# Cosine attention and highway layer: pair 5 and token tile 1 turned on TensorE, in a newly planned order

## The chip, the cores and the metric

The kernel runs on one core of a Trainium2 chip. The metric is the time of the whole kernel on the device in microseconds, the median of several runs. The engines are TensorE (PE in the profile; its weight loads are PEld), ScalarE (ACT), VectorE (DVE), GpSimd (POOL) and SyncE (SP), and 16 DMA engines move data.

## The reference

For 8 batches of 12 heads, 448 positions and 64 dimensions, queries and keys are divided by their norms, the scores divided by tau = 0.1 go through a softmax, and the result weighs v. The heads are then put side by side to 3584 tokens of 768 numbers, and a highway layer follows.

```python
q_n = q / (np.linalg.norm(q, axis=-1, keepdims=True) + 1e-06)
k_n = k / (np.linalg.norm(k, axis=-1, keepdims=True) + 1e-06)
scores = np.matmul(q_n, k_n.transpose(0, 1, 3, 2)) / tau
attn = softmax(scores)
x = np.matmul(attn, v).transpose(0, 2, 1, 3).reshape(3584, 768)
H = np.maximum(x @ w_h, 0.0)
T = 1.0 / (1.0 + np.exp(-(x @ w_t + b_t)))
out = T * H + (1.0 - T) * x
```

## The kernel before, in words

**Pairs and tiles.** Work is cut into 48 head pairs (pair n belongs to batch n // 6; heads n % 6 and n % 6 + 6 of it) and 28 token tiles of 128 tokens (three for each batch, and one more for every two batches, made of the last 64 positions of both). For each batch k, q and v are loaded by GpSimd's DMA with a cast to fp16 (names l, r, v, x; tiles raw, vf, vp). For batch 0 the first two pairs come sooner: as fp32, into the tile fa, by the queues of SyncE and ScalarE (op `fa`). The squares (`sq`, lines 607 and 608, on ScalarE or VectorE), the sums (`f1`, `f2`, `red`) and an inverse square root by VectorE (`nw`) give the factors. The products with them (`nm`, lines 667 and 668) write qkn, one instruction for each half of a pair, on VectorE or GpSimd.

**The turn of a pair.** For the scores a pair must lie with the dimensions in the partitions (qkT). There are two ways: seven transposes on TensorE into PSUM (`pt`, line 683) and a copy by ScalarE or VectorE (`cp`, lines 692 and 694), or one DMA transpose in SyncE's queue (`tr`, line 699). A token tile is turned in the same two ways before its matmuls with w_h and w_t: six transposes (`xp`, line 840) and a copy (`xc`, lines 848 and 850), or a DMA transpose (`xt`, line 832). The list CHOICES says which: 1 for TensorE, 0 for DMA. Its first 48 entries are the pairs, the other 28 the tiles.

**The rest of a pair.** Four groups of score matmuls (`qk`, lines 739 and 742), four exps on ScalarE (`ex`, lines 756 and 758), 32 matmuls with v (`av`, line 779; `vc`, lines 715 and 716, has spread v before), and the division on VectorE (`un`, lines 787 to 793) into xb, or st for the last 64 positions, which two small DMAs then bring into xl (`sh`). A tile's matmuls are `ff` (lines 864 and 867, two halves for each weight), then `d`, `t`, `g`, `h`, `e` and `o` combine them and `st` stores. The weights are loaded as halves `w00`, `w01` (w_h) and `w10`, `w11` (w_t).

**Fillers.** In the first microseconds there is nothing to multiply. Filler matmuls of 128x512 (line 485) on a constant tile zf keep TensorE busy; FILLS gives how many stand in each place (`fill0`, `fill1`, ...). The first two places together open the program.

**The order.** All ops are listed with `add`, and each has a number by its place in that list. QUEUES holds, for each engine, the numbers of its ops in the order in which it runs them, so that every instruction waits behind those before it. This order was made ahead of time by a planner (class Planner), which estimates how long an op takes, when a load lands and which buffers are free; the estimates for a DMA are the five entries of `dma`: its class, the number of units, the time of one, and the times before and after. HOLDS says for some of the loads which pair's first scores must have run before they begin. In the kernel before, some numbers are: pt0 207, pt1 212, tr5 234, qk5_0 527, av5 535, xt1 982, w00 to w11 22 to 25. With four places for fillers more, all later numbers rise by four.

In the order before, PE runs ... av3, qk5_0, qk4_2, qk4_3, av2, qk5_1 ..., and SP runs fa, the load of b_t, tr5, xt1, the first store, tr12 ... After the first two pairs' squares ScalarE takes one piece of batch 0's squares and copies pair 1, while VectorE copies pair 0 and squares the other piece.

Of the kernel before, what the change touches and what calls it, by code (L numbers as in the profile page):

```python
# [19 lines left out]
FILLS = [9, 23, 2, 8, 1, 1, 3, 6, 1, 1, 1, 1, 3, 1]  # L20
# [4 lines left out]
        1, 2, 207, 212, 3, 477, 479, 4, 487, 5, 489, 6, 481, 7, 491, 483, 8, 227, 493, 222, 485, 495, 217, 507, 517, 509, 9, 511,  # L25
        10, 497, 513, 11, 519, 12, 499, 13, 501, 503, 515, 527, 521, 523, 505, 529, 531, 533, 525, 242, 535, 547, 14, 237, 549,
        996, 965, 551, 553, 537, 247, 968, 539, 999, 541, 970, 557, 257, 543, 559, 561, 983, 252, 262, 972, 567, 985, 545, 569,
        555, 577, 987, 974, 579, 563, 571, 989, 587, 1001, 581, 573, 589, 565, 583, 591, 575, 593, 585, 595, 1003, 1042, 1005,
        1011, 1045, 597, 599, 1047, 1014, 601, 603, 607, 1049, 609, 617, 1016, 1030, 611, 619, 1032, 605, 647, 613, 621, 1018,
        1034, 649, 651, 1020, 1061, 623, 627, 629, 1063, 615, 637, 653, 639, 1036, 625, 631, 633, 641, 1051, 635, 677, 643, 657,  # L30
        655, 645, 659, 679, 1065, 1067, 1104, 661, 302, 681, 683, 322, 1107, 667, 663, 669, 1109, 665, 1111, 685, 687, 707, 1076,
        671, 673, 697, 1078, 709, 699, 675, 701, 703, 689, 1092, 1080, 711, 691, 693, 1094, 1082, 1096, 1098, 695, 1113, 713, 727,
        729, 705, 715, 737, 731, 733, 352, 1120, 1135, 747, 739, 735, 1138, 717, 719, 1140, 1123, 1125, 1127, 749, 721, 723, 1154,
        1129, 751, 757, 725, 767, 753, 1142, 1144, 741, 769, 743, 1169, 1171, 1173, 771, 773, 759, 1175, 1156, 761, 763, 745, 755,
        765, 775, 787, 789, 1158, 1182, 817, 777, 1197, 1160, 779, 819, 1185, 1200, 781, 797, 783, 1187, 1202, 791, 821, 1189,
        1216, 799, 801, 803, 785, 1218, 807, 809, 793, 1220, 1222, 811, 827, 795, 1191, 813, 829, 831, 805, 815, 887, 889, 823,
        1204, 833, 891, 825, 835, 837, 893, 839, 1206, 1244, 841, 843, 877, 895, 1247, 845, 1249, 857, 867, 1251, 1231, 847, 849,
        1253, 851, 853, 869, 1262, 859, 855, 871, 873, 861, 1278, 1280, 863, 879, 881, 1282, 1284, 865, 875, 883, 1264, 907, 909,
        885, 1233, 927, 929, 1235, 931, 933, 917, 1237, 919, 1266, 911, 921, 923, 1309, 1311, 1268, 913, 897, 899, 1293, 1295,
        947, 901, 903, 1297, 1324, 1299, 905, 915, 937, 939, 935, 949, 925, 941, 943, 951, 1313, 953, 945, 955, 1315, 1326, 1328,  # L40
        1330, 1355, 1357, 1340, 1342, 1344, 1371, 1346, 1359, 1361, 1373, 1375, 1377, 1386, 1388, 1391, 1393,
    ],
    "ACT": [
        29, 126, 134, 213, 478, 480, 488, 482, 445, 446, 490, 484, 492, 494, 228, 141, 518, 508, 510, 512, 498, 514, 520, 500,
        502, 504, 528, 522, 524, 530, 532, 534, 243, 548, 550, 966, 552, 554, 538, 540, 542, 558, 258, 560, 544, 253, 562, 973,
        451, 568, 155, 578, 988, 570, 975, 580, 564, 572, 990, 588, 582, 574, 590, 584, 453, 592, 594, 160, 1004, 164, 1006, 1012,
        598, 600, 602, 608, 604, 1050, 610, 618, 612, 620, 455, 622, 648, 1019, 1035, 614, 650, 1021, 652, 628, 624, 630, 638,
        640, 1037, 654, 632, 634, 1052, 642, 678, 644, 658, 458, 461, 680, 1066, 660, 1068, 662, 682, 684, 323, 664, 668, 173,
        670, 1112, 688, 708, 672, 698, 674, 710, 700, 702, 690, 704, 1081, 692, 712, 694, 1083, 1097, 1099, 1114, 714, 728, 730,
        738, 732, 734, 1136, 740, 748, 463, 718, 182, 720, 1128, 722, 724, 750, 1130, 752, 758, 464, 768, 1143, 754, 1145, 742,  # L50
        744, 770, 772, 1174, 1176, 774, 760, 762, 764, 187, 788, 790, 1159, 818, 778, 1198, 1161, 780, 820, 465, 466, 782, 798,
        792, 822, 784, 1190, 800, 802, 804, 467, 808, 810, 1221, 469, 794, 812, 828, 1223, 1192, 814, 830, 832, 888, 824, 834,
        1205, 890, 892, 838, 894, 840, 1207, 1245, 842, 844, 878, 200, 868, 858, 1252, 848, 850, 1254, 852, 854, 870, 860, 872,
        862, 874, 864, 880, 1283, 882, 1285, 884, 908, 910, 928, 930, 1236, 932, 918, 1238, 920, 934, 922, 912, 473, 924, 1267,
        1269, 474, 898, 900, 914, 475, 1298, 902, 904, 1300, 948, 938, 940, 950, 942, 944, 952, 954, 1314, 1316, 1329, 1331, 1345,
        1347, 1360, 1362, 1376, 1378, 1387, 1389,
    ],
    "DVE": [
        0, 20, 18, 21, 27, 127, 128, 129, 138, 210, 205, 206, 211, 208, 130, 131, 135, 136, 132, 137, 133, 139, 140, 220, 225,
        226, 221, 16, 215, 223, 145, 447, 218, 486, 142, 146, 448, 143, 147, 144, 149, 240, 496, 148, 506, 516, 246, 235, 526,  # L60
        536, 449, 238, 150, 997, 248, 250, 969, 450, 260, 251, 971, 261, 1000, 984, 263, 452, 151, 986, 152, 546, 153, 156, 991,
        157, 556, 976, 992, 977, 154, 993, 158, 994, 159, 1002, 566, 576, 586, 596, 271, 1043, 290, 161, 1046, 280, 281, 162,
        1015, 286, 454, 1048, 1007, 1008, 1053, 1054, 1017, 163, 165, 1031, 166, 1033, 167, 606, 168, 1022, 1023, 305, 1024, 1062,
        456, 315, 1064, 1025, 316, 616, 1038, 626, 311, 1039, 1055, 1040, 1056, 636, 457, 459, 646, 656, 460, 301, 1105, 1069,
        303, 1070, 1108, 169, 1110, 170, 666, 171, 174, 172, 175, 1077, 1115, 176, 1116, 177, 1079, 676, 335, 1093, 336, 686,
        1084, 1085, 1095, 351, 325, 345, 341, 326, 1100, 696, 1086, 462, 1101, 1087, 1117, 706, 716, 1118, 353, 1121, 178, 1139,
        179, 1141, 180, 1124, 1126, 183, 181, 184, 185, 1155, 186, 355, 726, 736, 1131, 1146, 1148, 1147, 1149, 1170, 1132, 1172,
        360, 356, 1177, 1178, 1179, 1157, 371, 1180, 746, 756, 766, 776, 191, 1183, 192, 188, 189, 1162, 1163, 190, 193, 1186,
        194, 1188, 1201, 195, 1203, 1217, 411, 385, 390, 786, 1219, 468, 405, 470, 471, 796, 472, 386, 406, 1224, 806, 1193, 816,
        1194, 1208, 826, 1209, 836, 196, 1225, 1210, 1211, 1226, 1248, 846, 1250, 197, 198, 201, 202, 199, 1232, 1255, 1256, 1263,  # L70
        203, 856, 204, 1279, 1281, 421, 430, 425, 431, 426, 866, 876, 1265, 440, 886, 415, 896, 441, 416, 1239, 1234, 1286, 1240,
        1241, 1242, 1310, 1312, 1270, 1271, 1272, 1273, 1287, 1294, 1296, 476, 1288, 1325, 1301, 1302, 1303, 906, 916, 1304, 926,
        936, 946, 956, 1327, 1317, 1332, 1333, 1318, 1356, 1358, 1334, 1341, 1343, 1335, 1348, 1372, 1363, 1364, 1374, 1365, 1366,
        1349, 1350, 1379, 1380, 1381, 1390, 1392, 1394, 1395, 1396,
    ],
    "POOL": [
        15, 17, 30, 37, 34, 38, 35, 31, 36, 32, 33, 42, 94, 96, 95, 44, 39, 43, 40, 97, 41, 45, 98, 25, 46, 216, 230, 231, 23, 22,
        100, 99, 53, 245, 241, 49, 236, 19, 24, 51, 48, 255, 256, 52, 47, 50, 101, 54, 60, 57, 58, 102, 104, 55, 105, 61, 56, 59,
        103, 978, 62, 68, 265, 266, 275, 270, 276, 69, 291, 285, 1009, 63, 65, 64, 110, 295, 66, 296, 306, 300, 106, 107, 320,
        310, 108, 70, 74, 67, 321, 109, 112, 71, 73, 111, 1071, 75, 78, 340, 77, 330, 331, 350, 83, 113, 76, 84, 72, 1102, 346,  # L80
        79, 81, 114, 82, 370, 80, 86, 375, 85, 115, 365, 361, 376, 366, 1133, 380, 381, 116, 118, 93, 120, 119, 117, 1164, 121,
        410, 89, 87, 92, 395, 400, 90, 401, 91, 88, 396, 1195, 391, 1257, 122, 420, 435, 436, 123, 124, 125, 1319,
    ],
    "SP": [
        28, 26, 234, 982, 995, 269, 957, 274, 279, 958, 294, 1029, 284, 979, 289, 1060, 299, 309, 1010, 1041, 1026, 959, 314,
        1057, 1075, 319, 1091, 1072, 339, 334, 329, 344, 1153, 349, 960, 1103, 1168, 1088, 1119, 364, 379, 359, 374, 369, 1181,
# [297 lines left out]
def kernel(  # L384
# [35 lines left out]
    fa = pool_.tile([128, 28, D], FP32, name="fa", tag="fa")  # L420
# [32 lines left out]
    add = P.add  # L453
# [586 lines left out]
```

## Time and profile before

| | before |
|---|---|
| time, median of 3 runs | 281.58 us (280.13 to 282.31) |
| profiled run: time, span | 279.94 us, 278.2 us |
| mean granted TensorE clock | 0.975 |
| busy share PE, PEld, DVE, ACT, POOL | 92%, 55%, 79%, 75%, 47% |
| chain that ended last | PE 71%, DMA 13%, ACT 6%, DVE 4% |
| DMA | 42.97 MB, mean 154 GB/s |
| fillers on TensorE | 61 matmuls, 18.2 us |
| DMA turns of pairs and of tiles | 34 and 18 |

The span is the time from the first to the last instruction. A share of an engine's busy time is a mean over all stages, so it doesn't say which engine sets the end in one of them. The chain is followed back from the last instruction, at each step to what released it; a DMA piece in it runs from issue to landing. Matmul ends are modelled, so TensorE can show as busy while it is paced by something else.

### The profile page before, as it was taken

Reading aid. Unit: us, or ns where it says so; the run is one execution under the profiler, and the core shown is the slowest. Engines: PE = TensorE matmul, PEld = TensorE weight load, DVE = VectorE, ACT = ScalarE, POOL = GpSimd, SP = SyncE. Lnnn points to the kernel's source line nnn. Section 1 sums busy time; section 2 is a strip of 40 time slices with the busy share of each in tenths; the row PEclk is TensorE's granted clock in tenths of the full one; section 3 lists DMA queues with packets and bytes.
Section 4 is the critical chain, followed back from the end, with each engine's and each line's share of the span. In section 5 each row is a group of like instructions: output and inputs, shape, how many; then the busy total and the mean of one; then the engine's idle time right before and its main releaser. Section 6 shows DMA issues by size and latency. Waiting matters only on the chain.

```text
span 278.2 us, 7772 instructions
## 1 busy us (share of the span) xinstructions
PE 255.8 (92%) x3155; PEld 153.3 (55%) x3155; DVE 219.0 (79%) x514; ACT 207.9 (75%) x287; POOL 131.2 (47%) x165
## 2 busy tenths in 40 slices
PE   7499729999999799999999999899999999999991
PEld 3135317556755367555765566356655655676660
DVE  3698935978999769799988989887798886756583
ACT  2359927899998869999599889888999589682230
POOL 9944731994856658148570778384303500001000
PEclk9979986999999999999999999999999999999997
DMA  8999695799999999999999999999855987514533
GB/s 165 183 182 173 92 181 65 112 183 182 141 149 179 159 210 170 213 134 193 145 120 191 199 157 135 174 154 161 213 128 128 192 107 192 130 59 91 171 152 113
DMA packets 109925, 42.97 MB, mean 154 GB/s; under 512 B 102721, under 2 KB 106305, under 8 KB 109890
## 3 DMA queue, kind: packets, MB, share of 16 engines
q0 software_dynamic: 56896, 18.42, 64.1%
q1 hardware_dynamic: 52162, 23.61, 38.2%
q8 instruction: 24, 0.39, 0.6%
q10 hardware_dynamic: 832, 0.46, 0.6%
q14 instruction: 11, 0.09, 0.1%
HBM read 37.75 MB, written 11.01 MB: 175 GB/s over the span
## 4 chain that ended last, share of the span: by engine, by line
PE 71%; DMA 13%; ACT 6%; DVE 4%; issue 2%; SPq 1%; POOL 1%; DVEq 0%; ACTq 0%
PE pb L864 33%; PE pb L779 17%; PE sc L739 11%; DMA xT<-xb 4%; DMA qkT<-qkn 4%; ACT ex L756 4%; PE sl L742 3%; DMA xT<-xl 3%; PE pb L867 3%; PE pb L683 2%; DMA fa<-in_k_dram 2%; PE pb L485 2%; ACT sq L607 1%; DVE sq L608 1%; PE pb L840 1%
## 5 line engine op out<-in xcount | busy, mean ns | idle before, releaser
L756 ACT ACTIVATE ex<-sc 128x896 f16<-128x896 f32 x144 | 127.7, 930 | 25.0 <-PE sc L739 23.2
L864 PEld LDWEIGHTS <-xT 128*128 128x128 f16 x672 | 60.8, 98 | 52.2 <-issue 13.1
L864 PE MATMUL pb<-w_h,xT 128*128 128x384 f16 x336 | 61.9, 327 | 2.5 <-DMA xT<-xl 1.7
L864 PE MATMUL pb<-w_t,xT 128*128 128x384 f16 x336 | 64.0, 327 | 0.0
L668 POOL TENSOR_TENSOR qkn<-raw,rs 128x448 f16<-128x448 f16 x44 | 40.7, 938 | 44.0 <-DVE qkn L668 18.3
L739 PE MATMUL sc<-qkT 64*64 64x448 f16 x576 | 50.7, 374 | 7.8 <-DMA qkT<-qkn 5.7
L779 PEld LDWEIGHTS <-ex 128*128 128x128 f16 x1536 | 52.5, 98 | 9.1 <-issue 7.6
L779 PE MATMUL pb<-vp,ex 128*128 128x65 f16 x1536 | 56.0, 194 | 0.2 <-ACT qkT L692 0.2
L951 POOL TENSOR_TENSOR o<-d,xb 128x768 f32<-128x768 f16 x8 | 13.1, 1640 | 46.8 <-DVE d L943 19.0
L882 DVE SCALAR_TENSOR_TENSOR d<-pb,xb 128x384 f16<-128x384 f32 x48 | 26.5, 554 | 11.0 <-PE pb L864 9.8
L739 PEld LDWEIGHTS <-qkT 64*64 64x64 f16 x576 | 17.0, 105 | 30.2 <-issue 18.0
L668 DVE TENSOR_TENSOR qkn<-raw,rs 128x448 f16<-128x448 f16 x48 | 31.4, 685 | 0.1
L758 ACT ACTIVATE ex<-sl 128x448 f16<-128x448 f32 x48 | 26.8, 558 | 3.0 <-PE sl L742 3.0
L789 DVE TENSOR_TENSOR xb<-pb,rd 128x384 f16<-128x384 f32 x48 | 26.8, 558 | 1.6
L890 ACT ACTIVATE t<-pb 128x384 f16<-128x384 f32 x30 | 14.9, 498 | 14.5 <-PE pb L867 14.4
L607 ACT ACTIVATE sq<-raw 128x2688 f16<-128x2688 f16 (+1 forms) x9 | 21.5, 2386 | 3.5 <-DMA raw<-in_k_dram 3.5
L787 DVE RECIPROCAL rd<-pb 128x7 f32<-128x7 f32 x48 | 9.6, 200 | 15.5 <-PE pb L779 14.7
L922 DVE SCALAR_TENSOR_TENSOR pb<-pb,d 128x384 f32<-128x384 f32 x26 | 14.6, 561 | 6.5 <-ACT pb L890 6.4
L550 POOL DMA_DIRECT2D raw<-in_q_dram x16 | 13.4, 840 | 13.2 <-PE sc L739 12.7
L485 PE MATMUL pb<-zf 128*128 128x512 f16 x61 | 18.2, 435 | 1.5 <-DVE warm L480 1.5
L890 ACT ACTIVATE pb<-pb 128x384 f32<-128x384 f32 x26 | 12.7, 488 | 9.1 <-PE pb L867 9.1
L585 POOL DMA_DIRECT2D vp<-in_v_dram x16 | 11.0, 685 | 15.8 <-PE sc L739 15.0
(70 smaller groups left out, 286.5 us busy)
## 6 DMA issues: line engine op xcount, KB each, us to landing
out_dram<-o SPq DMA_DIRECT2D x24, 384.0 KB, 3.3
vf<-in_v_dram POOLq DMA_DIRECT2D x16, 288.0 KB, 6.4
raw<-in_k_dram POOLq DMA_DIRECT2D x14, 288.0 KB, 6.4
raw<-in_q_dram POOLq DMA_DIRECT2D x14, 288.0 KB, 6.9
out_dram<-o SPq DMA_DIRECT2D x8, 192.0 KB, 2.8
w_t<-in_moe_w_t_dram POOLq DMA_DIRECT2D x2, 576.0 KB, 7.3
w_h<-in_moe_w_h_dram POOLq DMA_DIRECT2D x2, 576.0 KB, 8.2
vp<-in_v_dram POOLq DMA_DIRECT2D x16, 48.0 KB, 5.2
```

The costliest lines, as they stand in the source:

```text
L485: nc.tensor.matmul(pb_r[key][:, 0:512], lhsT=zf[:, 0:128], rhs=zf[:, 0:512], start=True, stop=True)
L607: return nc.scalar.square(o, r)
L668: return eng.tensor_mul(qkn_r[n][:, :, g, :], raw_r[b][:, 42 * g + 7 * hn : 42 * g + 7 * hn + 7], rs_r[b][:, g, h].unsqueeze(2).to_broadca ...
L739: last = nc.tensor.matmul(sc_r[n, j][o, g, 0:S], lhsT=T[:, 128 * j + 64 * i : 128 * j + 64 * i + 64], rhs=rhs, start=True, stop=True)
L756: nc.scalar.activation(o, sc_r[n, j][:, :, 0:S], AF.Exp, scale=inv_tau / (NSC * NSC))
L758: nc.scalar.activation(ex[:, 3136 : 3136 + S], sl_r[n][:, 0:S], AF.Exp, scale=inv_tau / (NSC * NSC))
L779: nc.tensor.matmul(u[:, s * 65 : s * 65 + 65], lhsT=l, rhs=r, start=(m == 0), stop=(m == len(ms) - 1))
L789: nc.vector.tensor_tensor(out=xo, in0=u[:, 0:6, 0:D].rearrange("p (g i) e -> p g i e", g=2), in1=rd[:, 0:6].rearrange("p (g i) -> p g i", ...
L864: nc.tensor.matmul(pt[:, 0:MH], lhsT=xT[:, c, :], rhs=w_sb[w][:, c, ms], start=(c == 0), stop=(w == 0 and c == CC - 1))
L882: nc.vector.scalar_tensor_tensor(out=d_r[m][:, h], in0=pb_r[m, w, h][:, 0:MH], scalar=0.0, in1=xsrc()[:, ms], op0=ALU.max, op1=ALU.subtract)
L890: nc.scalar.activation(src if flat else t_r[m][:, h], src, AF.Tanh, scale=0.5)
L922: nc.vector.scalar_tensor_tensor(out=t, in0=t, scalar=1.0, in1=d_r[m][:, h], op0=ALU.add, op1=ALU.mult)
```

## The change

The turns of pair 5 and of token tile 1 go from DMA to TensorE, so that the first DMA turn is that of pair 12. The second filler place, which is the larger part of the opening block, gets 37 matmuls for 23, and the later places are redistributed, 68 fillers in all for 61. In the planner the tail of the first load (fa) is put at 3300 ns for 1400, since the load lands later than was assumed. With these the order of all engines and the holds of the loads were planned anew.

```diff
-FILLS = [9, 23, 2, 8, 1, 1, 3, 6, 1, 1, 1, 1, 3, 1]
+FILLS = [9, 37, 2, 1, 1, 1, 1, 1, 1, 1, 2, 2, 2, 3, 1, 1, 1, 1]
...
 CHOICES = [
-    1, 1, 1, 1, 1, 0, 1, 1, 1, 1, 1, 1, 0, 0, 0, 0, 0, 0, 0, 1, 0, 0, 0, 1, 0, 0, 0, 0, 0, 1, 0, 0, 0, 0, 0, 0, 0, 0, 0, 0, 0, 0,
-    0, 0, 0, 0, 0, 0, 1, 0, 1, 1, 0, 1, 0, 0, 0, 1, 1, 1, 0, 0, 1, 1, 0, 0, 1, 0, 0, 0, 0, 0, 0, 0, 0, 0,
+    1, 1, 1, 1, 1, 1, 1, 1, 1, 1, 1, 1, 0, 0, 0, 0, 0, 0, 0, 1, 0, 0, 0, 1, 0, 0, 0, 0, 0, 1, 0, 0, 0, 0, 0, 0, 0, 0, 0, 0, 0, 0,
+    0, 0, 0, 0, 0, 0, 1, 1, 1, 1, 0, 1, 0, 0, 0, 1, 1, 1, 0, 0, 1, 1, 0, 0, 1, 0, 0, 0, 0, 0, 0, 0, 0, 0,
 ]
...
-            f_op = add("fa", {"SP": (2400, 3000, 0.0, False)}, -20, f_fn, dma=("f", 48, 40, 1900, 1400), count=4)
+            f_op = add("fa", {"SP": (2400, 3000, 0.0, False)}, -20, f_fn, dma=("f", 48, 40, 1900, 3300), count=4)
```

QUEUES and HOLDS are replaced whole. By the names of their ops, the starts of the orders that matter here are these (before, then after):

```diff
 PE
-fill0 fill1 pt0 pt1 fill2 qk0_0 qk0_1 fill3 qk1_0 fill4 qk1_1 fill5 qk0_2 fill6 qk1_2 qk0_3 fill7 pt4 qk1_3 pt3 av0 av1 pt2 qk3_0 qk4_0 qk3_1 fill8 qk3_2 fill9 qk2_0 qk3_3 fill10 qk4_1 fill11 qk2_1 fill12 qk2_2 qk2_3 av3 qk5_0 qk4_2 qk4_3 av2 qk5_1 qk5_2 qk5_3 av4 pt7 av5 qk7_0 fill13 pt6 qk7_1 xp2 xp0
+fill0 fill1 pt1 fill2 pt0 fill3 qk1_0 fill4 qk0_0 fill5 qk0_1 fill6 qk1_1 fill7 qk1_2 fill8 qk0_2 fill9 pt3 qk0_3 fill10 qk3_0 qk1_3 qk3_1 fill11 pt2 fill12 pt4 qk3_2 fill13 qk2_0 qk3_3 fill14 qk2_1 pt5 av1 qk2_2 fill15 qk4_0 av0 qk2_3 fill16 qk4_1 fill17 qk4_2 av2 qk5_0 qk4_3 qk5_1 av3 qk5_2 qk5_3 pt7 av4 av5 qk7_0 qk7_1 pt8 xp0 xp1
 ACT
-warm sq0_0 sq0_4 cp1 ex0_0 ex0_1 ex1_0 ex0_2 vc0_00 vc0_01 ex1_1 ex0_3 ex1_2 ex1_3 cp4 sq1_0 ex4_0
+warm sq0_0 sq0_4 sq0_2 cp1 cp0 ex1_0 ex0_0 ex0_1 ex1_1 ex1_2 ex0_2 cp3 ex0_3 ex3_0 sq1_0 ex1_3
 POOL
-ident iex1 lk0_2_0 rq0_1 rk0_0 lk1_0_0 rk0_1 lk0_2_1 rq0_0 lq0_2_0 lq0_2_1 rk1_0 v0_0 x0_0 v0_1
+iex2 ident lk0_2_0 rq0_1 lq0_2_1 rk0_0 lk0_2_1 lq0_2_0 rq0_0 rk0_1 lk1_0_0 rk1_0 lq1_0_1 rk1_1 lk1_0_1
 SP
-fa bld tr5 xt1 st1 tr12 sh0 tr13
+fa bld tr12 sh0 tr13 xt4 tr14 tr15
```

## The prediction

> **What bounds the kernel now.** I read the page's shares first, then the chain of work that ended last in order of time, then the timeline around its longest single piece, then busy time by stretch. TensorE is busy 92% of the span, so over most of the run only less work or a better packing on it could help. The chain, however, has a DMA share of 13%. Its first minute holds the longest piece (columns: start, length, what):
>
> ```profile
> 29.41 0.95 POOL qkn L668
> 30.37 11.08 DMA qkT<-qkn
> 41.49 0.96 PE sc L739 x8
> 42.83 1.88 PE pb L779 x32
> ```
>
> The piece of 11.08 us is the DMA turn of one head pair. Line 699 issues its first DMA turn at 30.37, and of the first twelve pairs only pair 5 is turned there; all the others go through TensorE. What it held up is in the timeline (start, length, engine, line, operation; in brackets the idle time before it and what ended that):
>
> ```profile
> 30.37 1.35 SPq L699 DMA_TRANSPOSE qkT<-qkn  x1
> ...
> 41.49 0.96 PE L739 MATMUL sc<-qkT 64*64 64x448 f16 x8 [5.06 <-DMA qkT<-qkn]
> ...
> 42.20 1.73 ACT L756 ACTIVATE ex<-sc 128x896 f16<-128x896 f32 x2 [5.46 <-PE sc L739]
> ...
> 42.76 1.94 PE L779 MATMUL pb<-vp,ex 128*128 128x65 f16 x32
> ...
> 44.74 0.21 DVE L787 RECIPROCAL rd<-pb 128x7 f32<-128x7 f32 x1 [7.19 <-PE pb L779]
> ```
>
> TensorE stood for 5.06 us, ScalarE for 5.46 and VectorE for 7.19, all for this one transfer: nothing covers it, since PE's order puts the scores of pair 5 ahead of everything else. The stretches (length, busy time of each engine, granted clock, DMA share, GB/s) show that TensorE also came back slow:
>
> ```profile
> 10.00:14.50 4.50, 0.29 (x2) 0.00 (x0) 4.19 (x13) 1.38 (x1) 4.47 (x7) 1.00 1.70 182
> 14.50:17.50 3.00, 2.99 (x25) 1.31 (x26) 2.85 (x5) 1.50 (x3) 2.22 (x4) 0.63 1.71 183
> 17.50:28.00 10.50, 10.00 (x117) 5.43 (x114) 9.54 (x28) 8.64 (x12) 3.35 (x4) 0.94 1.45 176
> 28.00:36.40 8.40, 6.93 (x92) 3.56 (x88) 7.81 (x21) 8.40 (x11) 5.89 (x8) 1.00 0.77 111
> 36.40:41.50 5.10, 0.04 (x4) 0.01 (x3) 1.15 (x3) 0.34 (x1) 2.30 (x3) 0.77 1.36 174
> 41.50:48.70 7.20, 7.20 (x127) 5.17 (x127) 3.59 (x12) 5.23 (x7) 1.04 (x2) 0.69 0.62 69
> 48.70:56.00 7.30, 7.17 (x75) 3.80 (x71) 7.03 (x18) 6.32 (x8) 6.84 (x12) 1.00 0.84 117
> ```
>
> After the idle 4.2 us ending at 14.5 the clock was 0.63, after the idle 5.1 us it was 0.69. Between 28 and 36.4 ScalarE was busy all 8.40 us: until the stall ScalarE, not TensorE, sets the pace of the first six pairs. From 48.7 on TensorE does.
>
> **What the Trainium skill says.** "TensorE: Matmul & The Clock Gate", in its closing table (Why this matters for your kernels), asks for no TensorE gap over about 3 us, else the clock falls back to half. The trace agrees: both gaps above are longer, and 32 attention matmuls took 1.94 us after the second against 1.19 before it. "DMA: Bandwidth & Descriptors", section "Issuing engines are not separate DMA queues", says that transfers from all issuers run on the same 16 engines and interleave. The trace agrees: two loads of w_h were issued at 30.29 and 31.1, with 174 GB/s moving in the wait, and the turn landed after 11.1 us where the median of this line is 3.7. The first page's Part 4 puts a 128x128 transpose on TensorE at about 275 to 390 ns, to be copied out of PSUM; the trace has 219 ns (7 in 0.55 us at full clock), and I use the trace.
>
> **The change part by part.**
>
> *Pair 5 by TensorE.* Removed: one DMA turn and its wait. Added: 7 transposes, 0.55 us of TensorE, and one copy out of PSUM on ScalarE, 0.91 us (the 896-wide copy at 47.54). The transposes lie in the ScalarE-paced stretch, where TensorE also runs fillers, so they cost nothing there; the copy does cost. The transposes sit ahead of pair 1's attention matmuls in PE's order and wait for the normalised pair 5, of which GpSimd makes one half after the first w_h load. In the old order both halves were finished at 30.36, on GpSimd; now the other half is VectorE's, in the middle of its norms.
>
> *How soon the first six pairs can then end.* I count on ScalarE. Now its first exp starts at 17.22 and the last exp of pair 5 ends at 47.49: 30.3 us, with idle time of 1.38, 0.48, 5.46 and 0.97, together 8.3; so 22.0 us of work. In the new order the two copies of v (1.23 us for both) leave, and the copies of pairs 3 and 5 come in (2 x 0.91): 22.0 - 1.2 + 1.8 = 22.6. The start also moves: ScalarE now squares all of batch 0's other four pairs in two pieces (1.70 us each) and copies pairs 1 and 0 (0.91 each) before its first exp, 5.2 us in all. Now those loads landed at 13.12, behind one load of batch 1 (288 KB, 1.6 us at the 182 GB/s of that stretch), which is moved behind them. So they land between 11.5 and 13.1, and the first exp comes between 16.8 and 18.4; I take 17.8. That gives 17.8 + 22.6 = 40.4 without a wait. For waits I add 1.0: of today's four, the 5.46 and the 0.97 (cold scores after it) go with the turn, and the 1.38 fell behind 8 fillers of 2.49 us, where the new order has one to three at a place. The last exp of pair 5 then ends at 41.4 instead of 47.5: **6.1 us earlier**, between 4.5 (late loads, 1.5 us more of waits) and 7.5.
>
> *Tile 1 by TensorE.* Its DMA turn was issued at 49.51 and nobody waited for it visibly, so nothing is gained on the path. Added: 6 transposes, 0.42 us (half of the pair of tiles that took 0.84), in the stretch that TensorE paces, and a copy of 0.55 us on VectorE, which is 7.03 of 7.30 us busy there. I charge 0.4 and up to 0.9. One filler of about 0.35 us between pairs 7 and 6 goes; I leave it in the range.
>
> *Longer first filler block.* 14 more fillers at 0.213 us are 3.0 us; the block that ended at 10.29 will end at 13.3, ahead of the first normalised pair (second pair of products at 13.3, first transposes at 14.5). It delays nothing, and the clock should be full when the pairs start. This is worth the cold part of 14.5 to 17.5: 8 score matmuls 0.96 against 0.57 and 14 transposes 1.28 against 1.1, about 0.6 us of TensorE. I count nothing, because ScalarE's squares set the first exp.
>
> *The later landing in the planner.* It is a number in the model that made the order; no instruction has it. It acts through the order alone.
>
> *Loads.* Everything after the first six pairs comes some 6 us earlier, so loads must too. First use of w_h was at 52.1, and would be at about 47. Its second half now is issued after the scores of pair 3 and an x load, about 30; with the 1.44 MB queued together at 182 GB/s that is 8 us, so it lands near 39. w_t's second half follows the products of pair 7 on GpSimd, about 40, and takes the 7.8 us that a w_t load took: 48, for a use near 52. DMA ran at 69 GB/s from 41.5 to 48.7, so room is there.
>
> Sum: 6.1 - 0.4 - 0.1 (VectorE in that stretch) = 5.6 us. From 48.7 on the order changes in many small places but the work is the same; I carry the gain to the end. 281.6 - 5.6 = **276.0**.
>
> **The rivals.**
> *More than that:* later TensorE waits for turned tiles, 1.7 us before 97.4 and 0.7 us twice near 175 and 181, also go with the new order, 3.1 us: 272.9. For it: they hang on when DMA turns meet loads, and two fewer turns are queued. Against it: 33 of the 34 pair turns and 17 of the 18 tile turns by DMA stay.
> *Half is given back:* the later stages meet loads and turns sooner, with DMA at 182 GB/s from 56 to 70 already; a new wait of 3.5 us appears: 279.5. For it: turns took 8.2 and 9.2 us in later stages too. Against: TensorE has other work around most of them.
> *Slower:* the new order puts two later turns into load bursts with nothing to cover them, each like pair 5's 5.1 us: 276.0 + 10.2 = 286.2. Against it: only one such case exists in the present trace.
>
> **How the numbers follow.** Forecast 0.68, more 0.13, half 0.14, slower 0.05. Faster by over 1% means under 278.8: the first two and a fifth of the third, 0.84; within 1% the rest of the third, 0.11; slower 0.05. The range of 272.5 to 279.5 takes in the ends of the 6.1 (277.6, 274.6), the case of more and half of the given-back case; the upper case and a little below are left out.
>
> **What would show it.** Right: no TensorE wait over 2 us between 15 and 45; last exp of pair 5 near 41.4; granted clock 1.0 throughout from 14 us on; first exp between 16.8 and 18.4; first w_h matmul near 47. Wrong: a wait for qkn in front of pair 5's transposes, ScalarE idle for the loads of batch 1 at its square near 25, a wait for w_h, or the 6 us present at 45 and lost again in TensorE waits behind 55.

## The result, and the profile after

The changed kernel takes 273.03 us (median of four, 272.43 to 277.8) against 281.94 us before: a ratio of 0.9697, with a 95% interval of 0.9632 to 0.9763. Executions of one kernel fall into a quicker and a slower group: the ratios and intervals here compare the quicker ones alone, and the medians take in all. The profiled execution spans 271.5 us against 278.2. The forecast was 276.0 in a range of 272.5 to 279.5.

The stretches of the changed kernel, with the bounds used for before (length, busy time of PE, PEld, DVE, ACT and POOL, granted clock, DMA share, GB/s):

```profile
10.00:14.50 4.50, 4.38 (x21) 1.77 (x19) 4.02 (x15) 2.13 (x2) 4.50 (x7) 1.00 1.66 166
14.50:17.50 3.00, 2.53 (x26) 1.27 (x26) 2.93 (x7) 3.00 (x4) 1.24 (x2) 1.00 1.69 174
17.50:28.00 10.50, 8.53 (x71) 3.78 (x68) 9.60 (x29) 10.46 (x13) 5.80 (x7) 1.00 1.45 157
28.00:36.40 8.40, 8.19 (x145) 5.15 (x144) 7.11 (x20) 8.40 (x12) 6.88 (x9) 1.00 1.20 160
36.40:41.50 5.10, 5.10 (x127) 4.18 (x124) 4.83 (x14) 4.28 (x7) 5.09 (x7) 1.00 1.31 197
41.50:48.70 7.20, 7.03 (x77) 4.30 (x75) 5.81 (x15) 7.20 (x10) 6.66 (x10) 1.00 1.40 190
```

The stretch in which all stood (36.4 to 41.5) is full, and the clock is 1.00 in every row, where before had 0.63, 0.94, 0.77 and 0.69 in four of them. ScalarE (the fourth busy time) is practically without a gap from 14.5 to 36.4 (21.86 of 21.90 us). Lines of its timeline, and TensorE's first matmuls with a token tile:

```profile
17.22 4.97 ACT L756 ACTIVATE ex<-sc 128x896 f16<-128x896 f32 x6
...
38.95 0.58 ACT L758 ACTIVATE ex<-sl 128x448 f16<-128x448 f32 x1
...
43.95 1.14 PE L864 MATMUL pb<-w_h,xT 128*128 128x384 f16 x6
```

The 38.95 row is the last exp of pair 5: it ends at 39.53, 7.96 us ahead of the 47.49 of before. The first token tile starts 8.2 us earlier (52.11 before). But the span is only 6.7 us shorter, so 1.3 us of this were lost again. TensorE's waits (in total, times, longest) say where:

```profile
PE pb L864 <- DVE o L928: 2.7, 1, 2.7
PE sc L739 <- DMA qkT<-qkn: 2.1, 2, 1.7
PE sc L739 <- DVE vp L716: 1.0, 1, 1.0
```

The first is at 86.7 us and the long one of the second at 137.1. Before had three waits over 0.5 us after 60 us (1.75, 0.67, 0.70, together 3.1). The changed kernel has none of these, but two larger ones (2.75 and 1.69, together 4.4).

The traces thus account for 6.7 us. The medians differ by 8.9, since the profiled execution of before (279.94 us) was 2.0 quicker than its median, and that of the changed kernel (273.25) was close to its own.

### The profile page after: what moved, and what is told of

The parts are those of the page before. It is cut to its first block, busy times and chain, and to the rows that moved or that the text cites. A ratio compares the mean times of both kernels' runs of the same rounds, so it can differ in the third digit from the quotient of the medians.

```text
span 271.5 us, 7806 instructions
## 1 busy us (share of the span) xinstructions
PE 255.7 (94%) x3175; PEld 152.9 (56%) x3175; DVE 221.6 (82%) x523; ACT 209.2 (77%) x286; POOL 126.0 (46%) x159
## 4 chain that ended last, share of the span: by engine, by line
PE 74%; DMA 12%; ACT 7%; POOL 2%; DVE 1%; SPq 1%; issue 1%; DVEq 0%; ACTq 0%; POOLq 0%
PE pb L864 38%; PE pb L779 16%; PE sc L739 11%; DMA qkT<-qkn 5%; PE sl L742 3%; PE pb L867 3%; ACT ex L756 2%; DMA out_dram<-o 2%; ACT sq L607 2%; DMA raw<-in_k_dram 2%; DMA vf<-in_v_dram 2%; ACT qkT L692 1%; POOL raw L550 1%; PE pb L840 1%; PE pb L683 1%
## 5 line engine op out<-in xcount | busy, mean ns | idle before, releaser
L951 POOL TENSOR_TENSOR o<-d,xb 128x768 f32<-128x768 f16 x5 | 8.2, 1638 | 52.1 <-DVE d L943 52.1
L739 PEld LDWEIGHTS <-qkT 64*64 64x64 f16 x576 | 16.2, 104 | 25.5 <-issue 17.2
L607 ACT ACTIVATE sq<-raw 128x2688 f16<-128x2688 f16 (+1 forms) x10 | 23.0, 2306 | 2.9 <-DMA raw<-in_k_dram 2.9
L485 PE MATMUL pb<-zf 128*128 128x512 f16 x68 | 20.4, 431 | 1.6 <-DVE warm L480 1.5
L890 ACT ACTIVATE pb<-pb 128x384 f32<-128x384 f32 x26 | 12.8, 492 | 10.4 <-PE pb L867 10.2
L867 PE MATMUL pb<-brow,ones 128*128 128x384 f16 x56 | 18.3, 326 | 0.0
L742 PE MATMUL sl<-qkT 64*64 64x448 f16 x96 | 17.6, 356 | 0.1
```

What stands on the lines that cost most here:

```text
L607: return nc.scalar.square(o, r)
L739: last = nc.tensor.matmul(sc_r[n, j][o, g, 0:S], lhsT=T[:, 128 * j + 64 * i : 128 * j + 64 * i + 64], rhs=rhs, start=True, stop=True)
L742: nc.tensor.matmul(sl_r[n][r, 0:S], lhsT=T[:, 832:896] if g == 0 else T[:, 384:448], rhs=rhs, start=True, stop=True)
L867: nc.tensor.matmul(pt[:, 0:MH], lhsT=ones[:, :], rhs=brow[:, ms], start=False, stop=True)
L890: nc.scalar.activation(src if flat else t_r[m][:, h], src, AF.Tanh, scale=0.5)
```

## The experiments

Twelve runs in three lots, each beside the kernel before on the same chip, whose medians were 281.48 (A to D), 282.33 (E to H) and 281.99 us (H again to L). "Last exp" is the end of the last exp of pair 5 in the profiled execution; it tells the early part apart from what follows. Runs A to D have line numbers one (A, B) or two (C, D) higher than the others.

| run | median (lowest-highest), us | ratio, interval | last exp |
|---|---|---|---|
| before | 281.94 | | 47.49 |
| the change | 273.03 (272.43-277.8) | 0.9697, 0.9632-0.9763 | 39.53 |
| A: before, pair 5 on TensorE | 277.87 (275.55-280.62) | 0.9826, 0.9771-0.9881 | 42.41 |
| B: before, w_h loads later | 280.42 (277.5-285.35) | 0.9932, 0.9885-0.9979 | 41.53 |
| C: change, pair 5 by DMA | 278.35 (270.82-280.01) | none | 39.12 |
| D: change, 23 fillers | 276.53 (274.56-277.76) | 0.9816, 0.9777-0.9855 | 39.94 |
| E: the change again | 272.80 (271.11-276.63) | 0.9666, 0.9607-0.9724 | 39.14 |
| F: A, 37 fillers, 1 for 8 | 278.04 (275.76-284.3) | 0.9852, 0.9814-0.9891 | 40.63 |
| G: change, stores early | 272.02 (269.06-273.93) | 0.9580, 0.9485-0.9675 | 39.03 |
| H: G and turn 24 earlier | 269.27 (268.24-270.37) | 0.9559, 0.9508-0.9610 | 39.06 |
| H again | 270.05 (268.75-272.54) | 0.9595, 0.9547-0.9644 | 39.07 |
| J: H, 23 fillers | 273.28 (272.36-275.25) | 0.9704, 0.9660-0.9748 | 40.73 |
| K: H, tile 1 by DMA | 271.00 (270.09-273.25) | 0.9636, 0.9591-0.9680 | 39.46 |
| L: H, pair 5 by DMA | 271.67 (270.49-274.46) | 0.9664, 0.9608-0.9720 | 40.47 |

**A: pair 5 alone.**

```diff
 CHOICES: pair 5 0 -> 1
 PE    ... qk4_1
+pt5
 ACT   ... ex2_1
+cp5
 SP
-tr5
```

> The kernel before with pair 5 alone turned on TensorE (transposes after the second group of scores of pair 4, the copy on ScalarE behind an exp of pair 2); everything else in the old order. Theory W (the uncovered DMA turn is the bulk of the gain): the wait of 5.1 us and the slow clock after it go, 0.9 us of copy comes; the last exp of pair 5 ends near 42.5 instead of 47.5 and the time is 275.5 to 277. Rival O (the new order is the bulk): the old order has other waits of loads right behind, and the time stays above 279.

The last exp came at 42.41, as theory W had it, 5.1 us earlier than before; the time of 277.87 is about 1 us over its figure. Pair 5's turn alone gives 1.7% of the 3.0% (3.6 us by the medians). What is left to the change's 39.53 shows in ScalarE's timeline of A:

```profile
17.67 1.73 ACT L757 ACTIVATE ex<-sc 128x896 f16<-128x896 f32 x2 [0.48 <-PE sc L740]
21.05 0.92 ACT L757 ACTIVATE ex<-sc 128x896 f16<-128x896 f32 x1 [1.65 <-PE sc L740]
22.45 0.92 ACT L757 ACTIVATE ex<-sc 128x896 f16<-128x896 f32 x1 [0.48 <-PE sc L740]
```

ScalarE waits 2.6 us for scores here. The scores of the long wait come after the eight fillers in TensorE's order; the changed kernel has one row of six exps without a gap.

**B: the DMA turn kept, the loads out of its way.**

```diff
 POOL
 nm5_0 nm5_1
-w01 w00
 x1_0 v1_1 rq2_1 nm8_0 nm7_1
+w01 w00
```

> The kernel before with one thing changed: the two loads of w_h, issued just ahead of pair 5's DMA turn at 30.3, go behind two products of GpSimd, to about 38. Theory L (the turn was slow because it shared the 16 DMA engines with 1.15 MB of weight loads): the turn lands in 4 to 6 us instead of 11, the wait on TensorE falls below 1 us, and the time comes to 276 to 278, though pair 5 is still turned by DMA. Rival (the DMA turn is slow by itself): it lands after 9 us or more and the time stays within 1% of before.

The turn's time from issue to landing, as the view of its line gives it:

```profile
DMA to landing us min/median/max: 2.7/2.7/2.7
```

It took 2.7 us instead of 11.1 with nothing changed but the place of the two loads, so these made the turn slow: theory L is right on that, and the last exp came at 41.53. That they did it by sharing the 16 DMA engines fits, but B doesn't show it apart. The DMA engines were not idle meanwhile: from 31.3 to 34 they moved 85 GB/s, against 147 from 30.4 to 41.5 in before. The time is not what it expected, though. TensorE now waited for what had been moved:

```profile
48.07 1.14 PE L865 MATMUL pb<-w_h,xT 128*128 128x384 f16 x6 [1.74 <-DMA w_h<-in_moe_w_h_dram]
```

More waits followed (0.70 for a tile's turn, 0.80 for v, 2.56 for a turn at 96, 0.74 and 1.25 for turns at 123 and 182), and of the 6 us only 0.7% (1.9 us) stayed.

**C: the change with pair 5 put back to DMA.**

```diff
 CHOICES: pair 5 1 -> 0
 PE
-pt5
 ACT
-cp5
 SP    fa bld
+tr5
```

> The changed kernel with pair 5 alone put back to a DMA turn, first in SyncE's queue. Theory W in its strict form (a DMA turn there costs a wait of about 5 us in any order): 277 to 279. Rival O (in the new order the turn is asked for at 26.4 and the scores of pair 5 come at 35.7, with only one weight load ahead of it): the turn lands by about 34, nobody waits, 0.9 us of ScalarE copy is saved, and the time is within 1 us of 273.

The turn took 10.0 us, almost as slow as before, but it was asked for at 25.27 and TensorE waited only 0.91 us for it: the last exp came at 39.12. The times lie so far apart (one at 270.82, five from 276.7 to 280.01) that C decides nothing on the time, only on the early part. Its profiled execution, of 277.9 us, lost 3.54 us at 140 in a wait for another pair's turn. For this reason L repeats the edit on a later version.

**D: 23 fillers in the change.**

```diff
-FILLS = [9, 37, 2, ...
+FILLS = [9, 23, 2, ...
```

> The changed kernel with 23 fillers in the second place instead of 37. Theory A (ScalarE's squares and copies set the first exp): TensorE stands about 3.5 us and comes back at a granted clock near 0.65, the first exp stays at 17.2 to 17.6, and the time is within 1 us of 273. Rival C (the clock matters): the first scores come late, and the time is 1.5 to 3 us longer.

The last exp was 0.4 us later than in the changed kernel, near theory A, but the time was 276.53, 3.5 us over the changed kernel and beyond rival C's figure. TensorE stood idle for 2.97 us and came back slow:

```profile
14.27 0.93 PE L685 MATMUL pb<-ident,qkn 128*128 128x128 f16 x7 [2.97 <-DVE qkn L669]
```

The first exp came 5.8 us after the start of ScalarE's two squares of batch 0 (17.65 and 11.88), where E, the changed kernel run again below, took 5.0 (16.84 and 11.84). D is read together with J.

**E: the change again.**

> The changed kernel once more, so that what follows is compared on one chip. The runs so far spread by over 1%. Theory E (the early gain of 8 us is fixed, what is lost of it later depends on how late transfers fall): last exp of pair 5 at 39 to 40 again, time 271 to 277, and TensorE waits over 1 us behind 80 us again, though not all at the same places. Rival (the changed kernel is steady and only the edited ones lost): 272.4 to 273.5.

272.80 us and the same two late waits, 2.42 at 86.0 and 1.66 at 136.2. So they are no accident of one execution, against theory E's "not all at the same places"; and D's 276.53, on an interval that doesn't touch E's, is a real difference.

**F: A, with the longer opening block and one filler in place of eight.**

```diff
 (on top of A)
-FILLS = [9, 23, 2, 8, ...
+FILLS = [9, 37, 2, 1, ...
```

> The kernel before with pair 5 turned on TensorE, 37 fillers in the second place and one instead of eight ahead of the first scores of pair 1; the order is otherwise the old one. Theory F (of the 2.9 us by which the changed kernel is ahead of pair 5 alone at the last exp of pair 5, most is ScalarE waiting behind fillers and slow scores): ScalarE's waits between 17 and 23 fall from 2.6 us to under 1, the last exp of pair 5 comes at 40.3 to 41.3 and the time is 1 to 2 us below pair 5 alone. Rival N (the newly planned order as a whole is needed): 42 or later, and no gain over pair 5 alone.

The last exp came at 40.63, inside theory F's figure, 1.8 us ahead of A, and ScalarE's waits between 17 and 23 fell to 0.5 us. But most of the 1.8 has another source than theory F named. ScalarE's square before the first exp began at 13.84 (13.75 in A), and the first exp came at 16.29, where A's, in the lines above, came at 17.67:

```profile
16.29 2.54 ACT L756 ACTIVATE ex<-sc 128x896 f16<-128x896 f32 x3
```

So 1.4 us come from transposes and scores that were no longer slow, and from the first exp to the last only 0.4 is gained, as a new wait of 1.24 appears at 24.7. The time did not follow: 278.04 against 277.87 for A. The profiled execution took 282.0 us, well over its median, and lost 5.99 us at 94.9 to a turn of xl, in its chain:

```profile
84.09 10.79 DMA xT<-xl
```

Whether this took the gain in the other executions too is not shown.

**G: the two stores early; H: also pair 24's turn.**

```diff
 SP    fa bld
+st0 st1
 tr12 sh0 tr13 xt4 tr14 tr15 tr17
-st1
 sh1
-st0
 xt6
...
 tr25 tr26
-tr28
 tr27 tr24
+tr28          (H alone)
```

> The changed kernel with the stores of token tiles 0 and 1 asked for ahead of pair 12's turn (their results were there at 63.6 and 66.1, the stores went out at 80.1 and 77.3). Theory S (the 2.75 us wait of TensorE at 86.7, through VectorE, was for the output buffer that tile 0's store frees): that wait goes, no other one over 1 us comes up to 100 us, and the time is 2 to 3 us below the changed kernel on the same chip. Rival (the store only stood last; the stage is bound by something else): a wait of the same size is at the same place with another releaser, and the time is the same within 1 us.

> As the one with early stores, and pair 24's DMA turn ahead of pair 28's instead of behind it (TensorE waited 1.7 us for it at 137.1). Theory T (that turn stood behind one that is needed later): the wait falls to under 0.5 us, the time is 1 to 1.7 us below that of the early stores alone. Rival (the turn is late because of loads on the DMA engines): the wait stays over 1 us.

In the changed kernel tile 0's result was ready at 63.6 and its store stood in SyncE's queue behind five pair turns, a tile's turn, sh0 and sh1 and tile 1's store. The second line below, from the view of line 928, says what VectorE's instructions there, for which TensorE waited, had waited for themselves (in total, times): the stores. In H again both stores go out at once (the third line):

```profile
80.09 0.59 SPq L965 DMA_DIRECT2D out_dram<-o  x1
  DMA out_dram<-o: 3.3, 2
```

```profile
63.19 2.86 SPq L965 DMA_DIRECT2D out_dram<-o  x2
```

In G the wait at 86.7 is gone and none over 0.3 us comes between 40 and 133; the span of the profile is 2.7 us under E's (267.9, 270.6), as theory S had it. Three of G's executions (269.06 to 270.88) are all under E's shortest (271.11), and three (273.17 to 273.93) lie among E's, so by the medians G is only 0.8 us under E and the time confirms theory S in part. In H the wait of 1.7 for pair 24 is gone too, as theory T had it. Its 1 to 1.7 us are not shown: the profiled span is only 0.2 under G's (267.7), with four waits of 0.2 to 0.4 us that G doesn't have, and G's three shortest executions are close to H's. But all six of H (268.24 to 270.37) are under the shortest of E. H beats both kernels, by 4.4% against before. TensorE's waits in H again (the first is that of 27.6 us):

```profile
PE sc L739 <- DVE vp L716: 1.0, 1, 1.0
PE pb L864 <- DVE o L928: 0.9, 1, 0.9
PE sc L739 <- ACT qkT L692: 0.5, 1, 0.5
```

> The version with early stores and turn 24 ahead of turn 28 once more, as the base for the next three on one chip: 268 to 270.5, last exp of pair 5 at 39.0 to 39.5.

Its 270.05 is within that, 4.0% under before; one execution reached 272.54.

**J, K, L: the three parts of the change undone on H**, with the edits of D (J), of C (L), and for K:

```diff
 CHOICES: tile 1 1 -> 0
 PE
-xp1
 DVE
-xc1
 SP    fa bld
+xt1
```

> That version with 23 fillers instead of 37 in the second place. With 37 removed in the changed kernel itself the last exp of pair 5 came only 0.4 us later, but the time was 3 us longer, by longer waits behind 80 us. Theory A (the fillers are worth the 0.4 us and the rest was chance in the late waits): within 1 us of the base, late waits absent. Rival C (a late start of 0.4 us shifts the transfers for the worse): 2 to 3 us over the base.

(In D it was 14 of the 37 fillers that were left out, not all.)

J is 3.2 us over H again, on intervals that don't touch, a little beyond rival C's figure. The stretches 7 to 14 and 14 to 21 us, H again first, then J:

```profile
7.00:14.00 7.00, 6.35 (x30) 2.65 (x28) 4.96 (x17) 3.96 (x3) 6.51 (x10) 1.00 1.68 180
14.00:21.00 7.00, 6.06 (x53) 2.98 (x54) 6.69 (x20) 6.84 (x9) 3.02 (x4) 1.00 1.72 180
```

```profile
7.00:14.00 7.00, 3.90 (x19) 1.57 (x16) 4.82 (x17) 3.83 (x3) 6.39 (x10) 0.94 1.70 181
14.00:21.00 7.00, 6.55 (x37) 2.84 (x38) 6.72 (x19) 5.74 (x7) 3.13 (x4) 0.58 1.62 166
```

J's TensorE idles 3.52 us and then has a clock of 0.58, and ScalarE does 1.1 us less in the second stretch. Its timeline shows the path: the transposes are slow, ScalarE waits for them, and then for slow scores.

```profile
14.41 0.93 PE L683 MATMUL pb<-ident,qkn 128*128 128x128 f16 x7 [3.52 <-DVE qkn L667]
...
16.98 0.91 ACT L692 COPY qkT<-pb 128x896 f16<-128x896 f16 x1 [0.69 <-PE pb L683]
...
17.94 1.97 ACT L756 ACTIVATE ex<-sc 128x896 f16<-128x896 f32 x2
```

In H again the same seven transposes take 0.56 and the first exp is at 16.77. The last exp is 1.66 us later in J. The spans of the two profiles differ by 3.8 us, and TensorE's waits after 70 us show 1.5 of the other 2.1 (J has 1.13 for a pair's turn at 74.7 and 1.16 for v at 136.6). That the late start caused these waits is not shown: K below starts like H again, and its profile has 1.63 for v at 136.2. Rival C is right on the time; how the later part of it comes about stays open.

> That version with tile 1 turned by DMA, first in SyncE's queue. Theory N (nobody would wait for it, it only costs 0.42 us of TensorE and 0.55 us of VectorE): the time is 0 to 0.8 us below the base. Rival (the DMA engines are full near 41 us and the turn lands late): TensorE waits before the first matmuls with w_t or behind them, and the time is 1 us or more over the base.

K: the turn was issued at 41.52 and took 7.8 us; no wait for it stands in the trace. The median is 1.0 us over H again, but the intervals overlap (0.9591-0.9680, 0.9547-0.9644). Neither theory is confirmed: tile 1 on TensorE costs nothing that can be seen, and may gain up to 1 us. (K's profiled execution, of 272.65 us, is one of its longer ones.)

> That version with pair 5 turned by DMA again. In the changed kernel this brought the last exp of pair 5 to 39.1 with a wait of 0.9 us, and times from 270.8 to 280. Theory O (with the turn asked for ten us ahead it is as good as TensorE's): within 1 us of the base, wait under 1.5 us. Rival W (its landing varies with the loads, and what it delays comes back later): over 1 us longer, or a spread over 2%.

L: the turn, issued at 26.4, took ten microseconds again:

```profile
DMA to landing us min/median/max: 10.2/10.2/10.2
```

TensorE waited 1.22 us for it, and the last exp came 1.4 us later than in H again, of which 0.4 was there at the first exp (17.19 for 16.77). The median is 1.6 us over H again. The intervals overlap narrowly, so the sign is likely and the size uncertain. The 5.1 us that the same turn cost in the old order are not there.

## Why the prediction was right, and where it was off

**The main step held.** The uncovered DMA turn was named from the chain and the timeline; A alone takes 5.1 us out of the early part, and B shows that the loads of w_h beside it made it slow. The expectation that the stall would not come back is right in the form that TensorE waited at most 1.02 us between 15 and 45.

**How soon the six pairs end** was the step with the wrong size: 41.4 forecast, 39.53 measured. Of the three terms, the work was right (22.3 us measured, 22.6 forecast); the first exp came at 17.22 for 17.8; and the 1.0 us "for waits" was 0.05. The new order feeds ScalarE without a gap, which the order of the op names alone had not told.

**"It delays nothing ... I count nothing"**, on the longer filler block, was the step that failed. The block ended at 14.38 for the 13.3 forecast, still ahead of the first transposes at 14.75, so it delayed nothing; it was its gain that was missed. Leaving 14 of the fillers out costs 3.7 us (D against E) and 3.2 (J against H again) by the medians. The clock part was forecast rightly (clock full from 14 us on), but not the conclusion that ScalarE's squares hide it: the copies after the squares wait for the slow transposes, and the exps for slow scores. With the squares at the same time, the first exp comes 1.4 us later without the longer block in the old order (A and F), and 0.8 to 1.0 in the new (D and J, counted from the start of the squares). The rest of the 3.2 to 3.7 us comes later, by a way that stays open.

**Errors that cancel.** The forecast had the right side and too small a size, 5.6 us for 8.9, and 273.03 is only 0.5 us inside the lower end of its range. The early part gained 1.9 us more than forecast and late waits took 1.3 back, so the 6.7 us of the traces lie nearer to the 5.6 than either part. That is luck in part.

**"I carry the gain to the end"** was too simple. Early gain and end differ: 8.0 us became 6.7 in the profile, B lost most of its gain, and F's did not reach its time. The rival "half is given back" named part of the mechanism: a turn that is met sooner is there (1.69 us), but the larger wait, of 2.75, hung on stores, which no rival named; only 1.3 us were lost on balance, for its 3.5. The rival "more" gave 272.9, almost the time measured. The three waits that it named did go, but new ones of 4.4 us came for their 3.1, so its number came out by luck.

**Tile 1** was charged 0.4 us; K shows no such cost. **Loads**: w_h's second half was issued at 31.64 (30 forecast) and nobody waited for it; the first use came at 43.95 for 47, as the early part ended sooner.

**The parts don't add up**: by the medians pair 5's turn is worth 3.6 us in the old order (5.1 at the last exp) and about 1.6 in the new, where it could be asked for ten microseconds before its use. And F, which has pair 5 and the longer block in the old order, comes within 1.1 us of the changed kernel at the last exp (40.63, 39.53), but is only 1.5% under before in time, where the change is 3.0 and 3.3%. With tile 1 worth at most about 1 us (K), what is left for the other half is the newly planned order, above all its later part. That is by elimination only: no run takes this order apart.

## What to carry to other kernels

A transfer on the path is judged by what else moves while it is under way and how long ahead it is asked for, not by its median: the same turn took 2.7 us with the two weight loads moved away and 10 to 11 beside loads, and cost 5.1 us of the early part or about 1. After an early stall is taken out, look for the next buffer or queue that everything now meets sooner; here two stores that stood behind transfers of later pairs in one queue held back the gain, and no cost of moving them showed. When idle TensorE time ends just ahead of a stage, keep it filled even if another engine seems to set that stage, and measure each part on the version that is steady.

## What the runs showed of the hardware

Seven transposes took 0.56 us at full clock and 0.93 us after an idle time of 3.52 us (J) or 2.97 (D), and in J the granted clock was 0.58 on average over the 7 us from 14 to 21. The Trainium skill ("TensorE: Matmul & The Clock Gate", closing table, Why this matters for your kernels) gives about 3 us of idle time for this fall, and the runs agree: the idle times of 0.4 to 1.7 us ahead of the same transposes in the change, H again, K and L left the clock full. The fall needn't show at once: in before, after 4.22 us of idle time, the first half microsecond of work still had the full clock, and 0.50 came a microsecond after the return.

```profile
14.50:15.00 0.50, 0.49 (x7) 0.39 (x7) 0.49 (x1) 0.31 (x1) 0.50 (x2) 1.00 1.78 178
15.50:16.00 0.50, 0.50 (x4) 0.24 (x3) 0.50 (x2) 0.17 (x1) 0.50 (x1) 0.50 1.65 183
```

Pair 5's DMA turn took 2.7 us with the loads of w_h moved away (B) and 11.1, 10.0 and 10.2 beside loads (before, C, L). Its issue in SyncE's queue took 1.33 us in B, and 2.5 and 2.9 in C and L; but in before it took 1.35, though that turn was the slowest, so a long issue is no sure sign of a slow turn. Executions of one and the same kernel spread by over 3% in C and F, and by 0.8% in H and 1.4% when it was run again.
